# A decode block in float32: the tail of an early weight load, split into loads of unequal row counts

## The chip, the cores and the metric

The kernel runs on one core of one Trainium2 chip. Its time is device microseconds, the median of several runs: 374.23 us before the change (three runs, 374.15 to 375.01).

## The reference

Two tokens (B = 2) of width 448 go through a layer norm, then through grouped attention over a cache and, beside it, through a bilinear feed-forward; the two are multiplied and added to the input. All is float32.

```python
xn = layernorm(x)                                  # [2, 1, 448]
q = xn @ wq                                        # 16 heads of 256
k, v = cache                                       # 2 x 8 key/value heads x 4096 x 256
p = softmax(q @ k.T * 256 ** -0.5)                 # two query heads share a key/value head
s = (p @ v) @ wo                                   # wo: [4096, 448]
g = silu(((xn @ w_gate) * (xn @ w_up)) @ w_down)
out = x + s * g
```

The cache is 16 pairs of (batch, key/value head), each with 4 MB of keys and 4 MB of values, and each byte of it is used once. The weights are another 24 MB or so.

## The kernel before, in words

Everything comes in by DMA from one queue, SP's. There are two large buffers (`ring`, 128 rows of 64 KB each) and one smaller one (`slot`). The program is written down as a list of operations per engine (`flow`), each with the operations that it has to wait for; what is printed on an engine is its order.

- At the start `wq0`, `wgu`, `wdq` and the first keys are issued. `wdq` goes to `slot`.
- Then there are 14 loads `vk[i]`, alternating between the two ring buffers. Each has 128 rows of 16,384 columns: the values of pair i and the keys of pair i + 1. SP issues one when the scores that read the buffer's previous keys are done.
- Pairs are worked on in turns of two (`for first in range(0, LAST, B)`, a loop on PE). For each pair: softmax of the scores (`m`, `mx`, `p`, `pT`), values (`o`), and the scores of the next pair (`s`). At the end of a turn, `combine` and `turn` write the two heads' outputs to `oT` on DVE (L222 in the profile, as every recorded operation), and the next turn's `project` multiplies them with four blocks of `w_o` in `slot`.
- `w_o` has 32 blocks of 448 columns. The first 24 (`LATE`) are the early load `wo`: 128 rows of 10,752 columns, put into `slot` once the feed-forward is done with it. SP issues it behind `vk[1]`. The other 8 come with the last load, `last1`, behind the values of pair 15.
- The first turn's `turn` is made to wait for the early load (`flow.weights`), so that the loop on PE needs no wait of its own for it.
- The end: values of pair 15 arrive as two loads (6,144 and 2,048 columns), the last blocks of `w_o` as three (5, 2 and 1 blocks). PE does the values of pair 15, `combine`, and `project_last` over the 8 blocks; two DVE operations and the store of 128 x 112 end the kernel.

The function that issues loads is `issue` (with `plan`, which lists them). A load is cut by columns only: `cuts` gives the borders, and each piece takes all 128 rows.

Of the kernel before, what the change touches and what calls it, by code (L numbers as in the profile page):

```python
# [8 lines left out]
B, D = 2, 448  # L9
# [11 lines left out]
LATE = 24  # L21
# [2 lines left out]
WQ = 14 * 512  # L24
LEAD = 48
GROUP = 4 * D


class Flow:
# [196 lines left out]
def gated_decode_block(nc, x, first, vk, last0, last1, wq0, wdq, wo, wgu, out):  # L226
    flow = Flow(nc)
    PE, DVE, ACT, POOL, SP = [getattr(flow, e) for e in ("PE", "DVE", "ACT", "POOL", "SP")]
    names = iter(range(1000))
# [15 lines left out]
    slot = Ring("slot", [128, PART], 1, 512)  # L245
# [7 lines left out]
    def two():  # L253
        pairs.append(pairs.pop(0))
        return pairs[-1]

    def bank(name=None):
        return banks[name] if name else two()[:, 0]
# [6 lines left out]
    def issue(n=1):  # L265
        for names, place, src, cuts in todo[:n]:
            t = place()
            width = ROW if not names[0].startswith("w") else src.shape[1] // len(names)
            for i, name in enumerate(names):
                loaded[name] = t[:, i * width:(i + 1) * width]  # L270
            if names == ["wd", "wq1"]:
                loaded["wd"], loaded["wq1"] = t[:, :14 * D], t[:, 14 * D:]
            for lo, hi in zip(cuts, cuts[1:]):
                SP.dma_start(t[:, lo:hi], src[:, lo:hi])
            if names == ["wo"]:
                flow.weights = len(flow.ops) - 1
        del todo[:n]

    def plan(names, place, src, cuts=None):
        todo.append((names.split(), place, src, cuts or [0, src.shape[1]]))  # L280
# [8 lines left out]
    for i in range(LAST):  # L289
        plan(f"v{i} k{i + 1}", ring, vk[i])  # L290
        if i == 1:
            plan("wo", lambda: slot()[:, GROUP:GROUP + LATE * D], wo)
    plan(f"k{LAST + 1} v{LAST}", ring, last0, [0, ROW, 2 * ROW])
    plan(f"v{LAST + 1} wo2", ring, last1, [0, 6144, ROW, *(ROW + i * D for i in (5, 7, 8))])
    issue(4)


# [128 lines left out]
    def query_of(i):  # L426
        g, b = divmod(i, B)
        return qT[g // 4][:, b, g % 4].rearrange("p d r j -> p d (r j)")

    def scores(i, q, s, halves=(0, 1)):  # L430
        k = loaded[f"k{i}"].rearrange("p (h d c n) -> p h d c n", h=2, d=2, c=NT)
        for h in halves:
            for d in range(2):
                for c in range(NT):
                    PE.matmul(s[W * c:W * (c + 1), h, :], q[:, d], k[:, h, d, c, :], start=d == 0, stop=d == 1)
        return s
# [19 lines left out]
    def exponential(i, s, m, mx):  # L456
        sm = bank("sm")
        PE.transpose(sm[:, 128:129], mx.rearrange("p c j -> p (c j)"), one)
        DVE.tensor_scalar(m[:, 1:2], sm[:, 128:129], -1.0 / 16, None, op0=OP.mult)
        p = work["p"]()  # L460
        ACT.activation(p, s, AF.Exp, bias=m[:, 1:2], scale=1.0 / 16, accum_out=su[:, i % B:i % B + 1])
        return p
# [5 lines left out]
    def softmax(i, s):  # L468
        m = peak(s)
        return turned(exponential(i, s, m, peak_of_all(m)), work["pT"]())  # L470
# [4 lines left out]
    def total(add):  # L475
        sm = bank("sm")
        PE.matmul(sm[:, :B], add.rearrange("p a r j -> p (a r j)"), su, start=True, stop=True)
        DVE.reciprocal(over, sm[:, :B])

    def values(i, pT, o):  # L480

        for e in range(KB):
            h, t, at = e // 8, e % NT, e % 8 * 2 * W
            PE.matmul(o[W * t:W * (t + 1), :], pT[:, h, at:at + 2 * W:2],
                             loaded[f"v{i}"][:, e * 512:(e + 1) * 512], start=e < NT, stop=e >= KB - NT)

    def combine(ob):
        cb = bank("cb")
        src = ob.rearrange("p s (e d c k) -> p s e d c k", e=2, d=2, c=NT)
        for e in range(2):  # L490
            for c in range(NT):
                PE.matmul(cb[W * c:W * (c + 1), :B * 64], add_blocks[:, e].rearrange("p r j -> p (r j)"),
                                 src[:, :, e, :, c, :], start=e == 0, stop=e == 1)
        return cb[:, :B * 64]

    def turn(oT, g, cb):
        DVE.transpose(oT[:, g].rearrange("p d r (b j) -> p b d r j", b=B),
                      cb.rearrange("p (b d r j) -> p b d r j", b=B, d=2, r=REP))
# [5 lines left out]
    def heads(i):  # L504
        return (oT if i < 28 else oT2)[:, 0, i % 2, i % 4 // 2]

    none = slot.bufs[0][:, :GROUP]

    def project(turn):
        for c in range(NT):  # L510
            at = turn * GROUP + c * D

            def call(c=c):
                block = slot.bufs[0][:, bass.ds(flow.index * GROUP + c * D, D)]
                return nc.tensor.matmul(wide[:W, :D], heads(c), block, start=False, stop=True, skip_group_check=True)  # L515

            flow.record("PE", call, [wide[:W, :D]], [heads(c), slot.bufs[0][:, at:at + D]])
# [20 lines left out]
    for first in range(0, LAST, B):  # L538
        flow.turn = first
        issue(2)  # L540
        if first == 0:
            flow.turn = None
            issue()
            flow.turn = first
        for i in range(first, first + B):
            p = softmax(i, s)
            o = bank("o")
            values(i, p, o)
            DVE.tensor_copy(ob[:, i % B], o)
            if i == first:  # L550
                project(first // B)
            q = copy()
            POOL.tensor_copy(q, query_of(i + 1))
            s = scores(i + 1, q, two())
        total(add_head)
        cb = combine(ob)
        t = work["h"]()[:, :B * 64]
        DVE.tensor_tensor(t.rearrange("p (s k) -> p s k", s=B), cb.rearrange("p (s k) -> p s k", s=B),
                          over[:, :, None].to_broadcast([128, B, 64]), op=OP.mult)
        turn(oT, 0, t)  # L560
        if first == 0:
            flow.ops[-1]["needs"].add(flow.weights)
    flow.turn = None
    issue(2)
    m = peak(s)
# [7 lines left out]
    p = exponential(LAST, s, m, mx)  # L573
# [5 lines left out]
    p = exponential(LAST + 1, late, m, mx)  # L579
# [65 lines left out]
```

## Time and profile before

| | |
|---|---|
| median of three runs | 374.23 us |
| the profiled execution, its own time | 374.16 us |
| span of the profiled execution | 372.5 us |
| DMA, mean over the span | 426 GB/s, 158.67 MB |
| busy: PE, DVE, ACT, POOL | 56%, 20%, 7%, 2% |
| mean granted TensorE clock | 0.784 of full speed |

The span lies within the execution; 1.66 us of the execution's time lie around it. The DMA share of the profile is the mean busy share of the 16 DMA engines of the core: a share of 0.19 is three of sixteen engines busy. A packet is what one engine moves in one go: one row of a load, or a 4-byte completion.

### The profile page before, as it was taken

What the parts mean: (1) busy time and instruction counts of PE and PEld (TensorE: products, weight loads), DVE (VectorE), ACT (ScalarE), POOL (GpSimd) and SP (SyncE); (2) the same over time, 40 slices, a digit from 0 to 9 for tenths busy, and PEclk for the clock granted to TensorE, in tenths of its full rate; (3) what the DMA queues carried; (4) which work ended last, traced back from release to release, by engine and by line L of the source; (5) the groups of instructions that cost most, each with busy time, mean ns of one, the idle gap of its engine ahead of it and who ended that gap; (6) DMA issues with size and microseconds to landing.
All of it is one profiled execution on the core that took longest, in us unless ns stands there. A gap on an engine that the chain in (4) does not pass through costs nothing. (4 is left out here: it accounts for less than half of the span.)

```text
span 372.5 us, 3409 instructions
## 1 busy us (share of the span) xinstructions
PE 208.9 (56%) x1482; PEld 64.9 (17%) x1482; DVE 75.9 (20%) x125; ACT 27.1 (7%) x47; POOL 8.3 (2%) x32
## 2 busy tenths in 40 slices
PE   0808392291900676458453838292819390948776
PEld 0101020030200121112121212030203130212222
DVE  2101023003130021302231122203130304030430
ACT  1101011001010001100100010101010101020120
POOL 2000100000000000000000000000000000000000
PEclk9968598597865596959695958697867786776999
DMA  8999999999999999999999999999999999999995
GB/s 343 456 436 404 436 426 450 450 438 396 430 457 450 429 450 429 415 415 450 450 429 450 429 415 415 450 450 429 450 429 415 415 450 443 436 405 440 410 422 238
DMA packets 4041, 158.67 MB, mean 426 GB/s; under 512 B 578, under 2 KB 708, under 8 KB 964
## 3 DMA queue, kind: packets, MB, share of 16 engines
q1 hardware_dynamic: 4032, 158.59, 98.6%
q8 instruction: 4, 0.07, 0.1%
q14 instruction: 1, 0.01, 0.0%
q10 hardware_dynamic: 4, 0.00, 0.0%
HBM read 158.54 MB, written 0.06 MB: 426 GB/s over the span
## 5 line engine op out<-in xcount | busy, mean ns | idle before, releaser
L222 PE MATMUL o<-ring,pT 128*32 128x512 f32 x480 | 82.6, 851 | 90.3 <-PEq L174 90.3
L222 PE MATMUL s<-ring,qc 128*32 128x512 f32 x448 | 55.7, 593 | 0.0
L222 PEld LDWEIGHTS o<-ring,pT 128*32 128x32 f32 x480 | 20.9, 150 | 139.3 <-issue 139.2
L222 ACT ACTIVATE p<-s,m 128x1024 f32<-128x1024 f32 x16 | 17.8, 1114 | 285.7 <-DVE m L222 285.7
L222 DVE COPY ob<-o 128x512 f32<-128x512 f32 x14 | 9.7, 692 | 132.2 <-PE o L222 132.2
L222 DVE TENSOR_REDUCE m<-s 128x1 f32<-128x1024 f32 x16 | 19.3, 1205 | 42.9 <-PE s L222 42.9
L222 PEld LDWEIGHTS s<-ring,qc 128*32 128x32 f32 x448 | 17.6, 109 | 30.5 <-issue 30.2
L222 DVE STREAM_TRANSPOSE pT<-p 128x1024 f32<-128x1024 f32 x15 | 18.7, 1245 | 19.1 <-ACT p L222 19.1
L515 PE MATMUL wide<-slot,oT 128*32 x56 | 22.2, 539 | 0.0
L222 PE MATMUL sm<-ident,m 128*1 128x128 f32 x16 | 4.4, 276 | 28.6 <-PEq L174 26.4
L222 PE MATMUL s<-ring,xnT 128*32 128x448 f32 (+1 forms) x72 | 11.9, 742 | 10.2 <-DMA ring<-wgu 10.2
L222 DVE TENSOR_REDUCE mx<-sm 1x128 f32<-1x512 f32 x16 | 10.9, 678 | 7.2 <-PE sm L222 7.2
L222 PE MATMUL sm<-one,mx 1*128 1x1 f32 x16 | 3.2, 201 | 12.8 <-PEq L174 12.1
L222 PE MATMUL s<-slot,hT 128*32 128x448 f32 x28 | 5.4, 887 | 8.0 <-DMA slot<-wdq 8.0
L222 POOL COPY qc<-qT 128x64 f32<-128x64 f32 x14 | 3.2, 237 | 256.4 <-PE s L222 256.4
L515 PEld LDWEIGHTS wide<-slot,oT 128*32 128x32 f32 x56 | 6.2, 110 | 15.8 <-issue 15.8
L222 PEld LDWEIGHTS sm<-ident,m 128*1 128x1 f32 x16 | 1.3, 79 | 38.3 <-issue 34.8
L222 PE MATMUL s<-ring,qT 128*32 128x512 f32 x64 | 7.5, 597 | 0.0
L222 PEld LDWEIGHTS s<-ring,xnT 128*32 128x32 f32 x72 | 3.1, 136 | 18.9 <-DMA ring<-wgu 11.1
L222 DVE RECIPROCAL over<-sm 128x2 f32<-128x2 f32 x8 | 1.4, 170 | 22.4 <-PE sm L222 22.4
L222 PE MATMUL cb<-ob,add_blocks 128*32 128x128 f32 x128 | 5.2, 279 | 0.8 <-ACT ob L222 0.8
L222 PE MATMUL s<-ident,pT 2*128 2x2 f32 x4 | 0.6, 246 | 8.6 <-DVE pT L222 8.6
(76 smaller groups left out, 72.0 us busy)
## 6 DMA issues: line engine op xcount, KB each, us to landing
ring<-last SPq DMA_DIRECT2D x2, 4096.0 KB, 24.8
slot<-wdq SPq DMA_DIRECT2D x1, 6720.0 KB, 41.5
ring<-wgu SPq DMA_DIRECT2D x1, 6272.0 KB, 25.3
slot<-wo SPq DMA_DIRECT2D x1, 5376.0 KB, 46.9
ring<-first SPq DMA_DIRECT2D x1, 4096.0 KB, 50.5
ring<-wq SPq DMA_DIRECT2D x1, 3328.0 KB, 11.0
ring<-last SPq DMA_DIRECT2D x1, 3072.0 KB, 21.1
ring<-last SPq DMA_DIRECT2D x1, 1120.0 KB, 23.7
```

What stands on the lines that cost most here:

```text
L222: self.flow.record(self.engine, lambda: method(out, *args, **kw), writes, reads, name == "dma_start")
L515: return nc.tensor.matmul(wide[:W, :D], heads(c), block, start=False, stop=True, skip_group_check=True)
```

## The change

The early load of `w_o` is cut at columns 9,912 and 10,352. The first piece, 9,912 columns, still takes all 128 rows. The next 440 columns come as one load of rows 0 to 55 and one of rows 56 to 127, the last 400 columns as one of rows 0 to 39 and one of rows 40 to 127. The wait of the first turn's `turn` is for all five loads.

```diff
+SHARES = {440: [(0, 56), (56, 128)], 400: [(0, 40), (40, 128)]}
...
+            begin = len(flow.ops)
             for lo, hi in zip(cuts, cuts[1:]):
-                SP.dma_start(t[:, lo:hi], src[:, lo:hi])
+                for p, q in [(0, 128)] if names != ["wo"] or not lo else SHARES[hi - lo]:
+                    SP.dma_start(t[p:q, lo:hi], src[p:q, lo:hi])
             if names == ["wo"]:
-                flow.weights = len(flow.ops) - 1
+                flow.weights = range(begin, len(flow.ops))
...
-            plan("wo", lambda: slot()[:, GROUP:GROUP + LATE * D], wo)
+            plan("wo", lambda: slot()[:, GROUP:GROUP + LATE * D], wo, [0, LATE * D - 840, LATE * D - 400, LATE * D])
...
-            flow.ops[-1]["needs"].add(flow.weights)
+            flow.ops[-1]["needs"].update(flow.weights)
```

SP's queue from the first keys on, before the change (`first` is the first keys, rows x columns behind the name):

```order
L222 DMA ring<-first 128x8192
L222 DMA ring<-vk 128x16384 [waits s9] x2
L222 DMA slot<-wo 128x10752
L222 DMA ring<-vk 128x16384 [waits s9] x12
L222 DMA ring<-last 128x8192 [waits s9] x2
```

The same place after it:

```order
L223 DMA ring<-first 128x8192
L223 DMA ring<-vk 128x16384 [waits s9] x2
L223 DMA slot<-wo 128x9912
L223 DMA slot<-wo 56x440
L223 DMA slot<-wo 72x440
L223 DMA slot<-wo 40x400
L223 DMA slot<-wo 88x400
L223 DMA ring<-vk 128x16384 [waits s9] x12
L223 DMA ring<-last 128x8192 [waits s9] x2
```

One load has become five in the same place; the order of the others is as it was.

DVE at the end of the first turn, before (`over` holds the softmax sums' inverses, `h` the outputs that `oT` gets transposed; `m` is the next pair's softmax; s11 counts the early load):

```order
L222 RECIPROCAL over<-sm 128x2 [waits s9]
L222 TENSOR_TENSOR h<-cb,over 128x128 [waits s9,s8]
L222 STREAM_TRANSPOSE oT<-h 128x2x4x16 [waits s11,s8]
L222 TENSOR_REDUCE m<-s 128x1
L222 TENSOR_REDUCE mx<-sm 1x128 [waits s9]
```

And after:

```order
L223 RECIPROCAL over<-sm 128x2 [waits s9]
L223 TENSOR_TENSOR h<-cb,over 128x128 [waits s9,s8]
L223 STREAM_TRANSPOSE oT<-h 128x2x4x16 [waits s15,s13,s14,s11,s12,s8]
L223 TENSOR_REDUCE m<-s 128x1
L223 TENSOR_REDUCE mx<-sm 1x128 [waits s9]
```

The one transpose that waited for the early load waits for five loads. No other engine's instructions change.

## Rows read from the trace of the kernel before

**Rows 1.** The page: DMA share in 40 equal slices, tenths

```profile
DMA  8999999999999999999999999999999999999995
```

**Rows 2.** The page: DMA queue, kind: packets, MB, share of 16 engines over the span

```profile
q1 hardware_dynamic: 4032, 158.59, 98.6%
q8 instruction: 4, 0.07, 0.1%
...
q10 hardware_dynamic: 4, 0.00, 0.0%
```

**Rows 3.** Chain that ended last, in order of time: start us, us, what

```profile
341.80 21.11 DMA ring<-last
...
362.94 3.69 PE s L222 x32
...
368.07 2.09 PE s L222 x64
```

**Rows 4.** Timeline of the end: start us, us, operation [idle before, releaser]

```profile
362.94 3.64 PE L222 MATMUL s<-ring,slot 128*32 128x512 f32 x32 [0.95 <-DMA ring<-last]
...
365.39 0.29 PEld L222 LDWEIGHTS s<-ring,slot 128*32 128x32 f32 x8 [0.57 <-DMA ring<-last]
...
368.07 0.92 PEld L222 LDWEIGHTS s<-ring,oT 128*32 128x32 f32 x40 [0.30 <-DMA ring<-last]
...
369.15 0.35 PEld L222 LDWEIGHTS s<-ring,oT 128*32 128x32 f32 x16 [0.16 <-DMA ring<-last]
369.72 0.16 PEld L222 LDWEIGHTS s<-ring,oT 128*32 128x32 f32 x8 [0.21 <-DMA ring<-last]
```

**Rows 5.** Stretches of the end; the last three columns are PEclk, DMA share, GB/s

```profile
368.00:368.20 0.20, 0.17 (x10) 0.13 (x9) 0.09 (x1) 0.00 (x0) 0.00 (x0) 1.00 0.51 197
368.20:368.40 0.20, 0.20 (x15) 0.20 (x15) 0.20 (x1) 0.00 (x0) 0.00 (x0) 1.00 0.80 243
368.40:368.60 0.20, 0.20 (x20) 0.20 (x15) 0.02 (x1) 0.00 (x0) 0.00 (x0) 1.00 0.25 99
368.60:368.80 0.20, 0.20 (x20) 0.20 (x14) 0.00 (x0) 0.00 (x0) 0.00 (x0) 1.00 0.19 72
368.80:369.00 0.20, 0.20 (x20) 0.19 (x9) 0.00 (x0) 0.00 (x0) 0.00 (x0) 1.00 0.21 81
369.00:369.20 0.20, 0.20 (x16) 0.05 (x7) 0.00 (x0) 0.00 (x0) 0.00 (x0) 1.00 0.18 72
369.20:369.40 0.20, 0.20 (x16) 0.20 (x16) 0.00 (x0) 0.00 (x0) 0.00 (x0) 1.00 0.08 27
```

**Rows 6.** DMA queues within 41 to 43 us: packets, MB, share of 16 engines

```profile
q8 instruction: 1, 0.02, 3.0%
```

**Rows 7.** DMA queues within 77 to 80 us

```profile
q8 instruction: 1, 0.02, 2.0%
```

**Rows 8.** DMA queues within 102 to 105 us

```profile
q8 instruction: 1, 0.02, 1.8%
```

**Rows 9.** A stretch of the middle; columns as in Rows 5

```profile
140.00:180.00 40.00, 23.18 (x158) 7.29 (x158) 9.31 (x14) 3.62 (x6) 0.47 (x2) 0.76 1.00 433
```

**Rows 10.** Timeline of SP's queue, 57 to 85 us

```profile
57.45 0.33 SPq L222 DMA_DIRECT2D ring<-vk  x1
57.82 0.44 SPq L222 DMA_DIRECT2D slot<-wo  x1
84.06 0.33 SPq L222 DMA_DIRECT2D ring<-vk  x1
```

**Rows 11.** Timeline of DVE and PE behind the early load

```profile
104.82 0.31 DVE L222 STREAM_TRANSPOSE oT<-h 128x128 f32<-128x128 f32 x1 [2.56 <-DMA slot<-wo]
...
109.32 1.25 DVE L222 STREAM_TRANSPOSE pT<-p 128x1024 f32<-128x1024 f32 x1 [1.27 <-ACT p L222]
```

**Rows 12.** Timeline of PE behind the early load

```profile
124.02 1.94 PE L222 MATMUL o<-ring,pT 128*32 128x512 f32 x8 [16.16 <-PEq L174]
```

## The prediction

> **What bounds the kernel now.** I read the page's slices first: the DMA engines are at eight or nine tenths from the first slice to the last but one [rows 1]. The page's queue list then says that one queue, SP's, moves 158.59 MB and holds 98.6% of sixteen engines over the span [rows 2], and a stretch of the middle shows a DMA share of 1.00 while PE works 23.18 of 40 us at a granted clock of 0.76 [rows 9]. So the kernel is as long as its loads take, plus a short tail. The chain of waits agrees: from 341.80 us on it hangs 21.11 us on the last loads, and only then on PE [rows 3]. The timeline of the end shows how tightly the tail follows: PE starts on the values of pair 15 at 362.94 us, after idling for their load, and its weight loads then wait 0.57, 0.30, 0.16 and 0.21 us for the four pieces behind it [rows 4]. An end of the loads that comes earlier by some tenths therefore shortens the whole by nearly as much, as long as all pieces move together.
>
> One engine moves 158.59 MB / (0.986 x 16 x 372.5 us) = 27.0 bytes per ns [rows 2]. What matters now is whether the sixteen finish together, and they don't. In the last stretches, in slices of 0.2 us, the share falls from 0.80 through 0.25 (four of sixteen engines) to 0.19, 0.21 and 0.18 (three) and 0.08 [rows 5]. So three engines work until about 369.3 us, a fourth until about 368.6, and the other twelve are done by about 368.4. A load has landed only when its slowest engine is done, so three late engines hold up every load.
>
> Why three? Beside the data there are four packets of instructions on a queue of their own, 16 KB each by the page [rows 2]. Three of them move in the first third of the kernel: 3.0% of 16 engines over 2 us is 0.96 us of one engine, 2.0% over 3 us again 0.96, 1.8% over 3 us 0.86 [rows 6 to 8]. Each holds one engine, which from then on is behind. Three fetches and three late engines fit, though the profile names neither the engines of the fetches nor the late ones.
>
> **The change: what each engine moves.** The last 840 columns of the early load are 8 rows x 840 x 4 = 26,880 bytes per engine, 26,880 / 27.0 = 1.00 us. How the new loads are shared out no row shows; the known cases bound it. A 128-row load makes 128 data packets and 16 completions, for 4,032 packets are 28 x 144 (27 loads and the store); a one-row load (the two of x) makes one data packet and one completion, 4 packets for two [rows 2]. In both, all engines in use have the same number of rows. I carry that on: 56 rows on 14 engines with 4 each, 72 on 12 with 6, 40 on 10 with 4, 88 on 11 with 8, the largest equal shares that sixteen engines allow. And I assume that the engines left out are taken from the same end each time. Then, with 1,760 bytes per row of 440 columns and 1,600 per row of 400:
>
> - two engines get nothing: 1.00 us less;
> - two get 4 rows, 7,040 bytes;
> - one gets 10 rows, 17,600 bytes;
> - one gets 18 rows, 30,400 bytes;
> - ten get 22 rows, 36,800 bytes.
>
> Small packets are slower than long ones. In two of the last slices, where only the final pieces of 1,792 to 3,584 bytes a row are left, the busy engines move 72 / (0.19 x 16) = 23.7 and 72 / (0.18 x 16) = 25.0 bytes per ns [rows 5]; I take 24.3 for the new packets. Against the 1.00 us of before, the five kinds come to -1.00, 7,040 / 24,300 - 1.00 = -0.71, -0.28, +0.25 and +0.51 us.
>
> [...]
>
> **What it does to the end.** If the three late engines are among the five relieved ones, they end 0.71 to 1.00 us earlier, at 368.3 to 368.6 us. Now others are last: the twelve that were done by 368.4 end by 368.9 where they carry the most, +0.51, and the fourth engine by 369.1 if it is one of them, earlier if it is relieved too. The end of the loads moves from 369.3 to between 368.6 and 369.1, that is 0.2 to 0.7 us earlier. I take 0.4, the case in which one of the twelve becomes the last. More than about 0.9 can't be had: after 368.0 us the sixteen engines have (0.51 + 0.80 + 0.25 + 0.19 + 0.21 + 0.18 + 0.08) x 0.2 = 0.44 us of work each on average [rows 5], so a perfect balance ends at 368.44.
>
> **What else it adds.** SP issues four loads more, at 0.33 to 0.44 us each [rows 10], 1.3 to 1.8 us in all. They stand between the early load's issue, over at 58.3 us, and the next issue at 84.06 us, for which SP waits for a buffer: 25.8 us of cover [rows 10]. Without that cover they would delay the load behind them by their own length. DVE's transpose waits for five loads in place of one. It waits 2.56 us now, and behind it DVE is queued with the next pair's softmax, whose last transpose starts at 109.32 and takes 1.25 us [rows 11]; who waits for that is PE's values, which start at 124.02, when their load has come [rows 12]. The 13.4 us between cover anything that the four waits or a landing half a microsecond later can cost. I put both at nothing.
>
> The sum is -0.4 us. Against the profiled execution, 372.5 us of span and 374.16 in all, this gives 373.76, and against the median of 374.23, 0.07 us above it, 373.83. I forecast 373.8 us.
>
> **Rivals.**
>
> *Nothing moves.* What is limited may be the place that is written to, not the engine that moves the packet. In every 128-row load each engine has rows of its own; a row of the last 840 columns that another engine carries still goes to the same place. If a place has fallen behind while its engine fetched instructions, and takes 27 bytes per ns and no more, it gets the same bytes as before and ends when it did: 374.2 us. For it: all engines run at one rate with a share of 1.00 [rows 9], which a limit on either side would give. Against it: a fetch goes elsewhere and still holds its engine for the full 0.96 us [rows 6]. The same result comes if the new loads are spread evenly over sixteen engines after all. [...] If places do limit and two engines hit one at once, the small packets run at half rate for a while: 22 of them cost some 1.5 us more on ten engines that had 0.9 us of room and lose 0.51 of it, so up to 1.1 us slower, 375.3.
>
> *Slower: the late engines are among the loaded ones.* It takes one of the three late engines among the ten that get 22 rows: that one then ends 0.51 us later than now, and with it every load, 374.7 us; with 18 rows, 0.25 later. For it: nothing in the profile names the late engines, and ten of sixteen is the larger part. [...]
>
> *A further fetch of instructions.* SP's list is longer by four; if that moves a fetch onto a late engine, another 0.9 us [rows 6 to 8], 374.7 with the gain taken off. Four fetches over the whole program [rows 2] make one more for a handful of instructions unlikely.
>
> **How the numbers follow.** The forecast case has 0.55 (373.5 to 374.1 as its own range), nothing moves 0.24, late engines among the loaded 0.15, and half-rate writes or a further fetch 0.06. About 0.3%, some 1.1 us, is what a measurement of this kernel can tell from no change, and all but the tails of these cases lie within it: the bound on the gain is 0.9 us, so faster by more needs something that I don't see, 0.06; slower by more needs half-rate writes or several losses together, 0.05; within it 0.89. The range is 373.2 to 374.8: the lower end is the bound on the gain, the upper the second rival.
>
> **What would show it.** Right: in the last stretches the stair of shares at a quarter and a fifth is gone or shorter, with many engines ending within half a microsecond; the values of pair 15 start about 0.4 us earlier than 362.94, and PE's waits behind them stay. If the stair keeps its length and its place, the first rival holds; if it is longer, with one to three engines at its end, the second. SP's four issues should stand directly behind the early load's at 58 us, and DVE's wait should end within half a microsecond of 104.8. A wait on the early load that reaches PE, or a gain above 1 us, would prove the reading wrong.

## The result: 375.88 us, slower by 0.38%

The changed kernel takes 375.88 us against 374.17 before (medians of five runs each), 1.71 us more. The ratio is 1.0038 with a 95% interval of 1.0026 to 1.0050; one of the five runs, 407.38 us, fell in a slow state and is left out of it. Forecast were 373.8 us and a range from 373.2 to 374.8. The profiled execution of the changed kernel takes 375.88 us, with a span of 374.6.

The page of the changed kernel, DMA by slice and by queue (packets, MB, share of 16 engines):

```profile
DMA  8999998999999999999999999999999999999995
...
q1 hardware_dynamic: 4335, 158.59, 98.5%
q8 instruction: 4, 0.07, 0.1%
q10 hardware_dynamic: 4, 0.00, 0.0%
```

The bytes are those of before, the share is 98.5 in place of 98.6%, the packets are 303 more [rows 2]. The four loads added make 56 + 72 + 40 + 88 = 256 data packets; the other 47 are completions (498 packets of 4 bytes in the trace against 451), and 14 + 12 + 10 + 11 = 47. That fits the shares that the prediction assumed, 14, 12, 10 and 11 engines. There are still four 16 KB fetches of instructions.

When the values of a pair arrive shows where the time went. PE starts on the values of a pair when their load has come: for pair 2, before the change, the sixteen landings of the load lie between 122.26 and 123.88 us, and PE starts at 124.02. For pairs 1 and 13, before the change (pair 2 is in [rows 12]; start us, us, operation, then idle before):

```profile
91.96 5.55 PE L222 MATMUL o<-ring,pT 128*32 128x512 f32 x32 [5.20 <-PEq L174]
...
336.40 6.21 PE L222 MATMUL o<-ring,pT 128*32 128x512 f32 x32 [4.44 <-PEq L174]
```

Pairs 1, 2 and 13 in the changed kernel:

```profile
92.31 6.53 PE L223 MATMUL o<-ring,pT 128*32 128x512 f32 x32 [4.12 <-PEq L175]
126.07 5.02 PE L223 MATMUL o<-ring,pT 128*32 128x512 f32 x32 [16.52 <-PEq L175]
...
338.45 6.34 PE L223 MATMUL o<-ring,pT 128*32 128x512 f32 x32 [4.30 <-PEq L175]
```

Pair 1 arrives ahead of the early load of `w_o`, 0.35 us later than before. Pair 2 arrives behind it, 126.07 - 124.02 = 2.05 us later. Pair 13, eleven loads on, is 336.40 to 338.45, again 2.05. So 1.7 us are lost between these two, in the stretch of the changed loads, and nothing is lost or won back behind it. (The 0.35 us arose before any changed load; the columns-only kernel below has 92.36 there and is no slower.)

That stretch, 101 to 107 us, with granted clock, DMA share and GB/s as the last columns, before:

```profile
101.00:107.00 6.00, 1.20 (x19) 0.62 (x19) 2.08 (x5) 0.00 (x0) 0.24 (x1) 0.93 1.09 467
```

And after:

```profile
101.00:107.00 6.00, 2.17 (x30) 0.81 (x22) 0.94 (x4) 0.00 (x0) 0.24 (x1) 0.83 1.07 332
```

The engines are as busy as before and move less: 467 / (1.09 x 16) = 26.8 bytes per ns and engine, then 332 / (1.07 x 16) = 19.4. Busy engines at 72% of their rate for 6 us lose about 1.7 us. So what costs the time is not idling: the packets take longer.

The trace also keeps every packet's start, duration and size. An undisturbed packet of a given size takes the same time in each kernel: 2.42 us for 64 KB, 1.47 for a row of the first piece, 73 and 67 ns for a row of 440 and 400 columns (the short ones from the columns-only kernel below). Over 88 to 130 us the changed kernel's packets take 27.0 us more than that together, 27.0 / 16 = 1.69 us per engine; before the change it is 0.04. Of the 27.0 us, 13.7 lie in the 64 KB packets of the load behind, 10.4 in the small rows and 2.6 in the first piece.

The end of the loads after the change, columns as in [rows 5]:

```profile
370.00:370.20 0.20, 0.20 (x12) 0.20 (x16) 0.00 (x0) 0.00 (x0) 0.00 (x0) 1.00 0.44 170
370.20:370.40 0.20, 0.20 (x19) 0.20 (x10) 0.00 (x0) 0.00 (x0) 0.00 (x0) 1.00 0.21 81
370.40:370.60 0.20, 0.20 (x20) 0.20 (x14) 0.00 (x0) 0.00 (x0) 0.00 (x0) 1.00 0.23 90
370.60:370.80 0.20, 0.20 (x20) 0.20 (x14) 0.16 (x1) 0.00 (x0) 0.00 (x0) 1.00 0.12 45
370.80:371.00 0.20, 0.20 (x20) 0.20 (x13) 0.15 (x1) 0.00 (x0) 0.00 (x0) 1.00 0.07 27
371.00:371.20 0.20, 0.20 (x20) 0.20 (x12) 0.00 (x0) 0.00 (x0) 0.00 (x0) 1.00 0.07 27
371.20:371.40 0.20, 0.20 (x20) 0.20 (x12) 0.00 (x0) 0.00 (x0) 0.00 (x0) 1.00 0.32 100
```

The stair is there still, some 2 us later, and its last step is one engine (0.07) in place of three. (The 0.32 of the last slice is mostly the fourth fetch of instructions, 0.88 us from 371.21 on.) In this execution PE itself is late too: at the scores of pair 15 the granted clock was 0.65 (349.8 to 354.7 us; 1.00 before, at 347.6 to 351.1), and the first 16 of their matmuls took 3.30 us in place of 1.92, so the chain of waits names PE to the end. That adds little, for in the kernel with two halves of the 840 columns, equally slow, PE waits for the last loads as before (below).

SP's and DVE's rows answer to [rows 10] and [rows 11]. SP in the changed kernel:

```profile
57.67 2.09 SPq L223 DMA_DIRECT2D slot<-wo  x5
85.45 0.36 SPq L223 DMA_DIRECT2D ring<-vk  x1
```

And DVE:

```profile
106.52 0.31 DVE L223 STREAM_TRANSPOSE oT<-h 128x128 f32<-128x128 f32 x1 [2.92 <-DMA slot<-wo]
```

Five issues take 2.09 us and have 25.7 us of cover; DVE's wait ends 1.7 us later than before, and PE's next values still come after idling 16.52 us. Neither holds PE up, as forecast.

### The profile page after: what moved, and what is told of

It is laid out like the page before. It is cut to its first block, busy times and chain, and to the rows that moved or that the text cites. A ratio compares the mean times of both kernels' runs of the same rounds, so it can differ in the third digit from the quotient of the medians.

```text
span 374.6 us, 3415 instructions
## 1 busy us (share of the span) xinstructions
PE 211.5 (56%) x1482; PEld 65.7 (18%) x1482; DVE 75.9 (20%) x125; ACT 27.1 (7%) x47; POOL 8.3 (2%) x32
## 3 DMA queue, kind: packets, MB, share of 16 engines
q1 hardware_dynamic: 4335, 158.59, 98.5%
## 5 line engine op out<-in xcount | busy, mean ns | idle before, releaser
L223 PE MATMUL o<-ring,pT 128*32 128x512 f32 x480 | 84.4, 868 | 90.4 <-PEq L175 90.4
L223 PE MATMUL s<-slot,hT 128*32 128x448 f32 x28 | 4.6, 764 | 8.9 <-DMA slot<-wdq 8.9
L223 PE MATMUL s<-ring,qT 128*32 128x512 f32 x64 | 8.9, 692 | 0.1
```

Of the source, the lines that this page charges most:

```text
L223: self.flow.record(self.engine, lambda: method(out, *args, **kw), writes, reads, name == "dma_start")
```

## Experiments

The theories. A: rows of the buffer belong to a limited number of places, each of which takes one engine's rate; when rows go in another grouping than 128 at a time, engines meet on a place and slow each other. B: a late engine is among those that carry more. C: narrow packets, added loads or loads of fewer rows cost by themselves. Others are named where they come up. Each kernel is compared with runs of the kernel before that were made beside it (medians 374.13 to 374.24 us).

**Cutting columns only.** `SHARES` becomes:

```diff
-SHARES = {440: [(0, 56), (56, 128)], 400: [(0, 40), (40, 128)]}
+SHARES = {440: [(0, 128)], 400: [(0, 128)]}
```

> The 840 columns are cut at the same two borders, but all three loads take 128 rows. Every engine moves the bytes it moved before, in three packets a row in place of one. Theory A (places: rows that are written by engines other than their own collide there): no rows change engine, 374.2 us, within 0.2. Theory B (bytes: some late engine is among the ten that got 22 rows): bytes are even again, 374.2 us. Theory C (the narrow packets, or the added loads and waits, cost by themselves): 0.5 us or more slower, 374.7 or above.

374.29 us, ratio 1.0003 (0.9994 to 1.0012). The stretch of before and after in this kernel:

```profile
101.00:107.00 6.00, 2.42 (x35) 0.89 (x23) 1.88 (x4) 0.00 (x0) 0.24 (x1) 0.84 1.03 433
```

433 / (1.03 x 16) = 26.3 bytes per ns and engine. Narrow packets and two loads and waits more cost nothing that can be measured.

**The 840 columns in two halves of 64 rows.**

```diff
-SHARES = {440: [(0, 56), (56, 128)], 400: [(0, 40), (40, 128)]}
+SHARES = {440: [(0, 64), (64, 128)], 400: [(0, 64), (64, 128)]}
```

> The same columns as loads of 64 and 64 rows, so that every engine again has the same bytes (4 + 4 rows of 440 columns, 4 + 4 of 400) in as many packets as the columns-only cut, but rows 0 to 63 are now written by all sixteen engines and then rows 64 to 127 by all sixteen. Theory A: each half goes to half of the places, so the 1.0 us that these columns take becomes up to 2.0: 374.5 to 375.3 us, and packets of 1,760 and 1,600 bytes take about twice their 73 ns. Theory B: 374.2 us, packets as short as before. Theory C: as slow as the columns-only cut.

375.92 us, ratio 1.0043 (1.0030 to 1.0057): as slow as the change, with the same bytes on every engine. So the loss needs no imbalance, and theory B isn't needed to explain it. Theory A had allowed only 375.3: it priced the small rows and not the wide ones beside them, and of the small rows only those of 400 columns slowed to 121 ns at the median, while half of those of 440 stayed at 73. The stretch of before and after in this kernel:

```profile
101.00:107.00 6.00, 1.11 (x22) 0.67 (x18) 0.46 (x2) 0.00 (x0) 0.24 (x1) 0.95 1.13 350
```

The rate is 350 / (1.13 x 16) = 19.4 bytes per ns, that of the changed kernel. PE's start on the values of pair 15, with its wait:

```profile
365.18 3.64 PE L223 MATMUL s<-ring,slot 128*32 128x512 f32 x32 [1.54 <-DMA ring<-last]
```

PE waits for the load, 2.24 us later than in [rows 4]: the whole loss arrives through the loads.

**The whole early load in two halves.** The columns stay in one piece.

```diff
-SP.dma_start(t[:, lo:hi], src[:, lo:hi])
+for rows in [slice(0, 128)] if names != ["wo"] else [slice(0, 64), slice(64, 128)]:
+    SP.dma_start(t[rows, lo:hi], src[rows, lo:hi])
...
```

> The whole early load, uncut in columns, as two loads of 64 rows: 0 to 63, then 64 to 127. Every engine moves the same bytes in the same 8 packets of 43,008 bytes as before. Theory A: each load writes to half of the places at half the rate, so the 12.7 us of the early load become about 25: some 12 us slower, 386 to 387 us. Theories B and C: no imbalance and no narrow packets, 374.2 us.

389.52 us, ratio 1.0409 (1.0393 to 1.0424): 15.3 us slower, more than the 12 expected. The stretch in which the two halves move:

```profile
92.00:118.00 26.00, 10.09 (x82) 3.21 (x82) 1.15 (x3) 0.00 (x0) 0.24 (x1) 0.70 1.03 222
```

All engines are busy at 222 / (1.03 x 16) = 13.5 bytes per ns. In the packets' own records a 43,008-byte packet takes 3.37 us at the median in place of 1.59. By theory A that is two engines on one place, which share a little less than one engine's rate (2 / 2.12 = 0.94).

**The whole early load as even and odd rows.**

```diff
-for rows in [slice(0, 128)] if names != ["wo"] else [slice(0, 64), slice(64, 128)]:
+for rows in [slice(0, 128)] if names != ["wo"] else [slice(0, 128, 2), slice(1, 128, 2)]:
```

> The whole early load as two loads of 64 rows: the even rows, then the odd rows. Packets, bytes per engine, number of loads and waits are those of the two halves; only which rows go together differs, and each load now touches all parts of the 128 rows. Theory A: all places are in use in both loads, so 374.2 us, and at most 1 us more where two engines still meet. Theories B and C: 374.2 us. If it is as slow as the two halves, 64 rows by themselves are slow and theory A is wrong.

378.17 us, ratio 1.0109 (1.0093 to 1.0124). Far less than the halves, but more than the 1 us allowed. SP's waits gave the reason:

```profile
SPq L222 <- DMA slot<-wo: 40.3, 1, 40.3
```

The list of dependencies sees an overlap between the even and the odd rows, and had SP wait for the first load; the DMA queue ran dry in between (the DMA share was 0.60, 0.37 and 0.57 at 94 to 97, 97 to 100 and 100 to 102 us; some 3 us). The packets' lengthening adds 0.7 us per engine: the first packets of the second load, which sixteen engines begin together, took 2.1 to 2.7 us, the later ones 1.59 again. Without that wait, with `op["needs"] -= set(flow.weights)` for the loads of the group:

> The even rows and the odd rows once more as two loads, without the wait that the kernel's own bookkeeping had put between them (the second load was issued only when the first had landed, and the DMA queue ran dry for some 3 us). Theory A: rows that go in this way do not collide, so nothing is left of the 3.9 us: 374.0 to 374.5 us. Theory C (loads of 64 rows cost something by themselves): 375 or more.

374.20 us, ratio 1.0004 (0.9995 to 1.0013), and every packet at 1.59 us:

```profile
101.00:107.00 6.00, 1.44 (x23) 0.75 (x19) 2.20 (x5) 0.00 (x0) 0.24 (x1) 0.97 1.12 481
```

That is 481 / (1.12 x 16) = 26.8 bytes per ns. Two loads of 64 rows are free if they are the even and the odd rows, and cost 15.3 us if they are rows 0 to 63 and 64 to 127.

**Read side or write side.** The buffer's halves, filled from even and odd rows of memory:

```diff
+for rows, of in ... [(slice(0, 64), slice(0, 128, 2)), (slice(64, 128), slice(1, 128, 2))]:
+    SP.dma_start(t[rows, lo:hi], src[of, lo:hi])
```

> The two loads of 64 rows once more, into rows 0 to 63 and then 64 to 127 of the buffer, but from the even and then from the odd rows of w_o in memory: this part of w_o arrives with its rows permuted. Theory A (the places that are written decide): as slow as the two halves, 389 to 390 us. Theory E (what decides is where the rows are read from): as fast as the even and odd rows, 378 us.

389.68 us, ratio 1.0411 (1.0395 to 1.0426); this part of `w_o` arrives with its rows permuted. The stretch in which the two halves move:

```profile
92.00:118.00 26.00, 10.19 (x82) 3.22 (x82) 1.16 (x3) 0.00 (x0) 0.24 (x1) 0.70 1.04 224
```

224 / (1.04 x 16) = 13.5 bytes per ns, as in the halves before. The rows written decide, not those read.

**The middle rows first.** Rows 32 to 95, then 0 to 31, then 96 to 127.

```diff
+for rows in ... [slice(32, 96), slice(0, 32), slice(96, 128)]:
```

> The whole early load, uncut in columns, as rows 32 to 95 in one load, then rows 0 to 31, then rows 96 to 127; each engine has 4 + 2 + 2 rows. Theory A says that rows are grouped into places and asks how. [...] If a place is eight rows in a row, the middle 64 rows too are 8 places and all is as slow as the two halves, 389 us. Theory C (loads of fewer than 128 rows are slow by themselves): at least as slow as the two halves. [...]

382.58 us, ratio 1.0223 (1.0207 to 1.0239). The two loads of 32 rows, 97 to 110 us:

```profile
97.00:110.00 13.00, 4.47 (x54) 1.57 (x46) 1.16 (x3) 0.00 (x0) 0.24 (x1) 0.82 1.03 230
```

Here 230 / (1.03 x 16) = 14.0 bytes per ns; the middle 64 rows ran at 1.59 us a packet. So 64 neighbouring rows can be fast, and which 64 they are decides (in the halves, rows 0 to 63 and 64 to 127 took 3.37 us a packet at the median); places of eight rows in a row are out. Which rows do share a place these runs don't show; the loads of 24 to 88 rows don't help, for how their rows are dealt out isn't known.

**Twice the columns.** 880 and 800 in place of 440 and 400, the row counts as in the change.

> The change with 1,680 columns in place of 840 (880 and 800), the same row counts. The engines that are left out get 2.0 us less, the ten others about 1.0 us more. Theory A (collisions decide, the relief is worth nothing): the loss of 1.7 us about doubles, 377 to 378 us. Theory D (the relief is real, and the loss is a fixed cost of the small loads): more relief, no more loss, 375 to 375.9 us. Theory B (bytes alone, a late engine among the ten): 0.5 us per 840 columns, 375.2 us.

377.29 us, ratio 1.0084 (1.0068 to 1.0099): 3.1 us slower, 1.8 times the change's 1.7. Twice the relief is no help, and the loss is no fixed cost (theory D, 375.9 at most).

**One part alone.** The 400 columns go back to 128 rows.

> Only the 440 columns are split by rows (56 and 72); the 400 columns behind them take 128 rows. Two engines are relieved by 0.52 us, two by 0.26, and twelve get 10 rows in place of 8. Theory A: part of the loss stays, 374.6 to 375.4 us. Theory D (a fixed cost per small load): half of the loss, 375.0. If it is 374.2 or below, the loss comes from the 400 columns alone, where the rows are shared most unevenly (40 and 88).

374.94 us, ratio 1.0015 (1.0006 to 1.0024). That is 0.8 us slower, about half of the change's loss, within theory A's range but also near the 375.0 of theory D; it is the doubled columns that speak against D. How the loss is divided between the two splits is not resolved by an interval of 0.2 to 0.9 us.

**Relief with spread rows.** Is less work for a late engine worth anything, if few engines meet?

```diff
-SHARES = {440: [(0, 56), (56, 128)], 400: [(0, 40), (40, 128)]}
+SHARES = [slice(0, 80, 2), slice(80, 128, 2), slice(1, 128, 2)]
...
```

The 840 columns stay in one piece here, and SP doesn't wait between the loads of the group.

> The last 840 columns as 40 even rows (0 to 78), 24 even rows (80 to 126) and 64 odd rows. By equal shares ten engines get 10 rows in place of 8, two get 6, and four get 4: the four are relieved by 0.5 us, the ten get 0.25 us more, and rows are spread so that few engines meet. Theory F (an engine that is behind catches up when it is given less): three late engines end 0.5 us earlier, 373.6 to 373.9 us. Theory A (what is behind is the place that is written, and it still gets all its bytes): 374.2 to 374.8 us.

375.03 us, ratio 1.0022 (1.0013 to 1.0031): slower and not faster, and 0.2 us above what theory A allowed. And with 1,680 columns:

> As the run before, with 1,680 columns: four engines are relieved by 1.0 us, ten get 0.5 us more. Theory F: the late engines end 1.0 us earlier, the next ones by 368.9, so 373.7 to 373.9 us. Theory A: no gain, and what collides is twice as much, 374.4 to 375.4 us.

376.45 us, ratio 1.0062 (1.0050 to 1.0074), more than the 375.4 that theory A allowed. The stretch of the small loads:

```profile
101.00:107.00 6.00, 1.65 (x26) 0.67 (x18) 1.18 (x4) 0.00 (x0) 0.24 (x1) 0.77 1.06 343
```

Again a full share at a lower rate, 343 / (1.06 x 16) = 20.2 bytes per ns. The records don't name engines, but an engine's next packet starts within some 10 ns of the end of the one before (within 4 ns for the 43,008-byte packets of before), so that single engines can be followed. The two that were last before the early load are among the four relieved. Their eight packets of the first piece took 11.4 and 11.6 us in place of 10.7, and their four remaining small rows 1.9 us in place of 1.0. They were spared 1.0 us and lost 1.6. For these two, theory F, that an engine catches up when it is given less, falls; by theory A their places get the same bytes, now from two engines at once. The times alone wouldn't have decided it: in the 840-column kernel the third late engine is a loaded one (its fetch at 102.63 us comes behind at least six small rows, and relieved engines have four). A kernel that relieves all three was not built.

## Why the prediction was wrong

- *What bounds the kernel* held: the loads, the stair of three late engines, the end that follows them. A load did land with its slowest engine: the early load's last packet ends at 104.09 us, the last of its sixteen landings is at 104.73, and the transpose that waits for it starts at 104.82 [rows 11]. Loads that end 2.05 us later (371.41 in place of 369.35) made the span 2.1 us longer. The three fetches as the cause of the stair held too: followed through the records of before, the three last engines are those with the fetches at 41.58, 77.90 and 102.67 us.
- *How rows are shared* fits the count of 47 completions. That the engines left out come from the same end each time was an assumption, and no record names an engine.
- *The late engines are among the relieved* held for two of the three only: in the changed kernel's packet records the last engine before the early load has four small rows and the next one none. The third, whose fetch comes at 107.01 us here, has a 1,600-byte row directly before its next load, so by the shares it carries 18 or 22 rows. It is the last engine of the whole kernel, at 371.41 us; the relieved two end at 370.63 and 370.16. So the second rival was true of this one, at a price of 0.25 to 0.51 us. How much of the 1.7 us that is no run separates; the kernel with two halves of the 840 columns has equal bytes on every engine and loses as much.
- *The step that failed* is "If the three late engines are among the five relieved ones, they end 0.71 to 1.00 us earlier". No late engine ended earlier, relieved or not. In the changed kernel the relieved two's eight packets of the first piece took 12.9 us each in place of 11.7: engines that were ahead had finished that piece and were, by theory A, already writing small rows into the late engines' places. What was spared later was lost before. The other three relieved engines ran ahead into the next load and had first packets of 3.9 to 4.0 us there in place of 2.42.
- *The second failed term* is +0.51 us for the ten loaded engines, taken from packets that had their place to themselves. The 1,600-byte packets took 131 ns at the median, 67 in the columns-only kernel. The engines with 18 or 22 rows were to end by 368.9; they ended between 369.7 and 370.9, and the late one among them at 371.41.
- The rival "nothing moves" had theory A's mechanism, and even its half-rate writes, but I priced these for the ten engines' small packets only and gave them a small part of 0.06. The price includes the wide packets that they collide with, on both sides of the small loads: 16.3 of the 27.0 us by which packets were longer. So it is 1.7 us, not 1.1. Rows of before could not settle it, for there every load has 128 rows. I weighed this rival against one fetch [rows 6], which says nothing of the write side. No record names the places it speaks of; what the runs show of half-rate writes is the halves' 13.5 bytes per ns and engine in place of 26.8.
- *Two readings were off without harm.* The share of 0.80 [rows 5] has the fourth fetch in it (1.26 us from 368.40 on, 0.39 of the share), so a perfect balance would end at 368.37 and not 368.44. And "0.71 to 1.00" is right for four of the five relieved engines; the fifth was to gain 0.28.
- SP's issues and DVE's wait cost nothing, and no further fetch came, as forecast.

That the rate depends on which rows are written together is shown: 13.5 bytes per ns and engine in the halves, 13.5 with the halves read from other rows of memory, 14.0 in the two loads of 32 rows, 26.8 in the even and odd rows, and 1.59 us a packet in the middle 64 rows as in the load of all 128. That engines meet on places which take one engine's rate each is theory A's reading of these rates. That the changed kernel loses its 1.7 us to packets made longer by such row cuts is shown by the columns-only kernel, the two halves of the 840 columns and the sum over the packets: 1.69 us per engine there, 1.8 in the two halves of the 840 columns, 15.2 in the halves of all, 0.04 for even and odd rows without the wait, each close to what the kernel lost. In the doubled kernel the sum is about 3.0 of 3.1 us, with an estimate of 126 ns for an undisturbed 3,200-byte row (3,360 bytes take 132 and 3,520 bytes 138). The two relief kernels with spread rows lose more than the sum (0.9 us against 0.6, and 2.3 against 1.7); the rest is not shown, the added rows of the loaded engines would be one cause. Which engine meets which on a place, and how the rows of a 64-row or 40-row load are dealt out, stays open.

## What to carry to other kernels

Here a load's speed depended on which rows it wrote: in the halves of the whole load the DMA share stood at 1.03 while each engine moved 13.5 bytes per ns in place of 26.8, so read the share together with the GB/s. Cutting a load by columns was free here (374.29 us); cutting it into rows 0 to 63 and 64 to 127 was not (389.52), nor were cuts at rows 40 and 56 (375.88); even and odd rows over the full height were (374.20). Giving a late engine's rows to others didn't help the two engines that could be followed, which were spared 1.0 us and lost 1.6 with 1,680 columns as spread rows: by theory A the rows still go to the same places. And ask of each late engine by itself whether a relief reaches it: here one of three got more work.

## What was not expected of the hardware

- Lateness stayed. Between pair 2 and pair 13 eleven loads of 8 MB pass and the changed kernel's 2.05 us neither grow nor shrink; the delay at 100 us was paid at the end, where the loads are over at 371.41 us in place of 369.35.
- A fetch of instructions cost its engine more than its own packet. The one at 41 us in the trace of before took 0.96 us [rows 6], and the 32 KB data packet behind it 1.67 us in place of 1.21: 1.4 us in all for 16 KB.
- In the halves of the whole load, where two engines share a place by theory A, most packets took 3.30 to 3.40 us (94 of 128), 6% more than twice the 1.59 of one alone; 17 packets took 3.09 to 3.13, 2% less than twice.
